# First-layer weights of an attention and two-FFN kernel: the shifted high word in a gapless tile of its own, joined with sign and low bits by one operation

## The chip, the core and the metric

One core of one Trainium2 chip. The metric is the device time of one execution in microseconds (us), with the median of three runs for the kernel before: 911.22 us (910.86 to 913.75).

## What is computed

Attention with 32 global and 512 local positions, 4 batches of 8 heads, a window of 32 around each local position; then two FFN layers on its 2176 rows of 512 columns:

```
x = attention(q_l, k_l, v_l, q_g, k_g, v_g)          # 2176 x 512
h = x @ moe_w_in;  x = (h * sigmoid(h)) @ moe_w_out  # 512 x 2048, 2048 x 512
h = x @ moe2_w_in; out = (h * cos(h)) @ moe2_w_out
```

The four weight matrices are float64 and have to become fp32 on the chip; the rest is fp32. Each fp32 product is made of three matmuls on a high and a low part of either operand.

## The kernel before

TensorE does each GEMM tile as `lo*xh`, `hi*xh`, `hi*xl` (`gemm1`, L491 to L493, into `ps_hid`; `gemm2` of the first layer, L558 to L560, into `ps_y`). The first layer works through tiles of tokens; tile 0 has 512 tokens and goes through 16 slices f of the hidden dimension. It needs all first-layer weights for the first time, so the conversion of these weights runs during tile 0: 32 chunks (16 slices, two parts each, 512 weights per partition), in the order in which the GEMMs want them. A chunk goes through these steps:

- `load_w1` (L113): a DMA brings 1024 words, low and high word of each float64 in turn, into a tile `raw`.
- `rebias` (L123): ScalarE multiplies the high words by a power of two in place (L125), so that a later shift by 3 gives the fp32 exponent; then it turns the low words into their top three bits, in place (L128). Both go over every other word.
- `to_f32` (L130): VectorE puts the sign of the high word into the low word (L136), then shifts the high word left by 3 and joins it with that (L140), into a gapless tile `w` out of the pool `stage`, tag "f", two buffers.
- `split_w_hi` (L153): ScalarE (L160) or, for the eight chunks in POOLED, GpSimd (L158) rounds `w` to the high part. `split_w_lo` (L163) subtracts on VectorE (L165), which frees `w`.

The weights of the second layer use the same two functions later, in chunks of 256, with one more shift on VectorE (L135). Tags "r" and "f" of `stage` (two buffers each) also hold those chunks' raw words, a batch's global values (`load_vg`, tag "f") and results on their way out (`finish`).

Beside the weights tile 0 carries the attention of further units of 256 positions: scores on TensorE (L243), masking and maximum on VectorE (L256, four instructions per unit, here called a **group**), exponentials on ScalarE (L266), transposes on VectorE (L196), global key parts on GpSimd (L202, L203), values on TensorE (`unit_values`, L335, L342). During tile 0 `gemm2` holds two of the four buffers `ps_a`, so one is free for a unit's values `ps_o` only when the group of the next unit has read its scores. Units 8 to 11 give four such groups in tile 0. VectorE also has `act` (L500) and `gl` (L535) for each slice f; ScalarE has the tanh (L499) and `gh` (L530).

The order of the work is a table of ticks (`at(rank, tick, function)`). From tick 0 to 35, which holds tile 0, a scheduler of the language puts each engine's instructions in order; before and after, they stand as recorded. Every engine works its own list in that order and waits in place.

Of the kernel before, what the change touches and what calls it, by code (L numbers as in the profile page):

```python
# [11 lines left out]
F32 = mybir.dt.float32  # L12
F32R = mybir.dt.float32r
I32 = mybir.dt.int32
U32 = mybir.dt.uint32
AF = mybir.ActivationFunctionType
ALU = mybir.AluOpType
# [23 lines left out]
ROUND = 12582912.0  # L41
REBIAS = 2.0**-112
SIGN = -(2**31)

TOP3 = 2.0**-29 * (1.0 - 2.0**-18)
TOP3_BIAS = -0.5 + 7.5 * 2.0**-18
# [3 lines left out]
def attention_then_two_ffn(  # L50
# [9 lines left out]
    nc = tc.nc  # L60
# [3 lines left out]
    stage = ctx.enter_context(tc.tile_pool(name="stage", bufs=2))  # L64
# [46 lines left out]
    W = {}  # L111

    def load_w1(f, part):  # L113
        raw = wts.tile([128, 1024], I32, tag=f"w{part}_{f}", name="raw")
        nc.sync.dma_start(out=raw, in_=w1[f, :, part * 1024 : part * 1024 + 1024])
        W[0, f, part] = raw.rearrange("p (n two) -> p n two", two=2)

    def load_w2_words(f, part):
        raw = stage.tile([128, 512], I32, tag="r", name="raw")
        nc.sync.dma_start(out=raw, in_=w2[f, :, part * 512 : part * 512 + 512])  # L120
        W[1, f, part] = raw.rearrange("p (n two) -> p n two", two=2)

    def rebias(ph, f, part):  # L123
        high = W[ph, f, part][:, :, 1].bitcast(F32)
        nc.scalar.activation(out=high, in_=high, func=AF.Copy, scale=REBIAS)  # L125
        if ph == 0:
            low = W[ph, f, part][:, :, 0]
            nc.scalar.activation(out=low, in_=low.bitcast(U32), func=AF.Copy, scale=TOP3, bias=TOP3_BIAS)  # L128

    def to_f32(ph, f, part):  # L130
        words = W[ph, f, part]
        n = words.shape[1]
        low, high = words[:, :, 0], words[:, :, 1]
        if ph == 1:
            nc.vector.tensor_scalar(out=low, in0=low, scalar1=29, scalar2=None, op0=ALU.logical_shift_right)  # L135
        nc.vector.scalar_tensor_tensor(  # L136
            out=low, in0=high, scalar=SIGN, in1=low, op0=ALU.bitwise_and, op1=ALU.bitwise_or
        )
        w = stage.tile([128, n], F32, tag="f", name="w")
        nc.vector.scalar_tensor_tensor(  # L140
            out=w.bitcast(I32), in0=high, scalar=3, in1=low, op0=ALU.logical_shift_left, op1=ALU.bitwise_or
        )
        W[ph, f, part] = w

    def store_w2(f, part):
        nc.sync.dma_start(out=w2f[f][part // 2][:, part % 2 * 256 : part % 2 * 256 + 256], in_=W.pop((1, f, part)))
# [449 lines left out]
    head, pre, gemm, pe, post = -20, 0, 10, 20, 40  # L596
# [6 lines left out]
    def begins(ph, t):  # L603
        return tick[seq.index((ph, t, 0))]
# [4 lines left out]
    def at(rank, i, fn, *args):  # L609
        plan.setdefault(i, []).append((rank, fn, args))  # L610
# [75 lines left out]
    for i, (need, f, part) in enumerate(chunks):  # L686
        s = min(need - SLACK, FIRST + i * (tick[NF] - 3 - FIRST) // (len(chunks) - 1))
        if i >= AHEAD:
            at(post, s - LOADS, load_w1, f, part)
        at(head + 6, s, rebias, 0, f, part)  # L690
        at(head + 7, s + 1, to_f32, 0, f, part)
        at(head + 10, s + 1, split_w_hi, 0, f, part)
        at(head + 6.5, s + 2, split_w_lo, 0, f, part)

# [3 lines left out]
    for i in range(4 * NF):  # L698
        s = free[i * len(free) // (4 * NF)]
        at(post, s - 2, load_w2_words, i // 4, i % 4)  # L700
        at(pre, s, rebias, 1, i // 4, i % 4)
        at(post - 1, s, to_f32, 1, i // 4, i % 4)
        at(pre, s + 1, store_w2, i // 4, i % 4)
    for f in range(NF):
        i = seq.index((0, len(SPANS) - 1, f))
# [6 lines left out]
    for i, (ph, t, f) in enumerate(seq):  # L712
        s = tick[i]
# [10 lines left out]
    for t, n in enumerate(size[1]):  # L724
        s = last if t == 0 else begins(1, t - 1)
# [19 lines left out]
    for n in range(5, EARLY):  # L745
        load_w1(*chunks[n - 5][1:])
        load_qk(n)
        load_v(n - 2)
    for n in range(EARLY - 2, EARLY):
        load_w1(*chunks[n - 3][1:])  # L750
        load_v(n)
# [90 lines left out]
```

## Time and profile before

| what | us |
|---|---|
| median of three runs (lowest, highest) | 911.22 (910.86, 913.75) |
| profiled execution, span from first to last instruction | 908.7 |
| TensorE matmul busy | 886.9 (98% of the span) |
| VectorE busy | 634.2 (70%) |
| ScalarE busy | 490.5 (54%) |
| GpSimd busy | 119.7 (13%) |

The page gives no time of the profiled execution beside its span; the median of the runs is 2.5 us above the span. Instruction rows of the trace give a start, a duration, and in brackets how long the engine was idle before and who ended that. An instruction of VectorE or ScalarE begins before the one ahead has ended, so what one costs is the distance from start to start, a little less than its duration. In tables of stretches PEclk is the granted TensorE clock as a share of full speed.

### The profile page before, as it was taken

How to read it: one execution, taken by the hardware profiler on the slowest of the kernel's cores; microseconds unless marked ns; L12 is line 12 of the kernel's file. 1: busy time of each engine (PE TensorE's matmuls, PEld its weight loads, DVE VectorE, ACT ScalarE, POOL GpSimd, SP SyncE). 2: the span in 40 equal slices, each digit the busy share in tenths (PEclk: the TensorE clock that was granted, in tenths of full speed). 3: DMA queues.
4: the chain of work that ended last, by engine and by line, in shares of the span. 5: the costliest groups of instructions: out<-in, count | busy, mean ns of one | idle time of the engine just before them, and what ended most of it. 6: DMA issues, size and time to landing. Idle time of an engine off the chain costs nothing.

```text
span 908.7 us, 15912 instructions
## 1 busy us (share of the span) xinstructions
PE 886.9 (98%) x5790; PEld 765.8 (84%) x5790; DVE 634.2 (70%) x1604; ACT 490.5 (54%) x1170; POOL 119.7 (13%) x147
## 2 busy tenths in 40 slices
PE   8899899999999999999999999999999999999998
PEld 5667678889888989999888889988889888888896
DVE  4799995688979677676488766666556656665654
ACT  4989843555644645444354465554445555444543
POOL 2220210021222212011155520000000000000000
PEclk9999989999999999999999999999999999999999
DMA  8968510566565664343546420000001000000100
GB/s 262 336 205 297 170 44 12 157 200 198 170 185 154 188 179 123 119 119 89 165 159 193 145 87 24 25 35 12 1 23 48 24 24 35 13 0 1 47 1 36
DMA packets 71839, 97.78 MB, mean 108 GB/s; under 512 B 22864, under 2 KB 38736, under 8 KB 71760
## 3 DMA queue, kind: packets, MB, share of 16 engines
q1 hardware_dynamic: 71760, 96.76, 34.3%
q8 instruction: 46, 0.75, 0.3%
q14 instruction: 33, 0.27, 0.1%
HBM read 79.43 MB, written 17.30 MB: 106 GB/s over the span
## 4 chain that ended last, share of the span: by engine, by line
PE 75%; DVE 10%; ACT 6%; DMA 2%; issue 1%; POOL 0%; SPq 0%; ACTq 0%; DVEq 0%
PE ps_hid L493 11%; PE ps_hid L491 11%; PE ps_hid L492 11%; PE ps_y L558 6%; PE ps_y L565 6%; PE ps_y L564 6%; PE ps_y L566 6%; PE ps_y L559 6%; PE ps_y L560 6%; PE ps_o L342 1%; DVE raw L136 1%; DVE gl L535 1%; PE ps_s L243 1%; DVE w L140 1%; ACT gh L530 1%
## 5 line engine op out<-in xcount | busy, mean ns | idle before, releaser
L493 PE MATMUL ps_hid<-xl,wt 128*128 128x512 f32 (+2 forms) x704 | 240.3, 341 | 0.0
L491 PE MATMUL ps_hid<-xh,wt 128*128 128x512 f32 (+2 forms) x704 | 240.2, 341 | 0.0
L492 PE MATMUL ps_hid<-xh,wt 128*128 128x512 f32 (+2 forms) x704 | 239.9, 341 | 0.0
L491 PEld LDWEIGHTS ps_hid<-xh,wt 128*128 128x128 f32 x704 | 133.0, 189 | 12.7 <-issue 0.4
L492 PEld LDWEIGHTS ps_hid<-xh,wt 128*128 128x128 f32 x704 | 133.0, 189 | 12.0
L493 PEld LDWEIGHTS ps_hid<-xl,wt 128*128 128x128 f32 x704 | 132.9, 189 | 10.3 <-DVE xl L355 0.3
L524 DVE TENSOR_TENSOR rest<-rest,ps_hid 128x384 f32<-128x384 f32 (+1 forms) x80 | 48.7, 608 | 132.8 <-ACT rest L520 132.7
L558 PE MATMUL ps_y<-gh,wt 128*128 128x256 f32 (+2 forms) x384 | 133.2, 347 | 0.0
L560 PE MATMUL ps_y<-gl,wt 128*128 128x256 f32 (+2 forms) x384 | 126.8, 330 | 0.3 <-DVE gl L535 0.3
L559 PE MATMUL ps_y<-gh,wt 128*128 128x256 f32 (+2 forms) x384 | 127.0, 331 | 0.0
L530 ACT CAST gh<-rest 128x384 fp32r<-128x384 f32 (+1 forms) x80 | 44.6, 558 | 122.4 <-PE ps_y L566 90.5
L564 PE MATMUL ps_y<-wt,gl 128*128 128x512 f32 x272 | 106.0, 390 | 1.7 <-DVE gl L535 1.7
L566 PE MATMUL ps_y<-wt,gh 128*128 128x512 f32 x272 | 106.7, 392 | 0.0
L565 PE MATMUL ps_y<-wt,gh 128*128 128x512 f32 x272 | 106.6, 392 | 0.0
L499 ACT ACTIVATE act<-ps_hid 128x256 f32<-128x256 f32 (+2 forms) x96 | 44.7, 466 | 89.6 <-PE ps_hid L493 89.5
L500 DVE SCALAR_TENSOR_TENSOR act<-act,ps_hid 128x256 f32<-128x256 f32 (+2 forms) x96 | 50.7, 528 | 56.3 <-ACT act L499 55.6
L558 PEld LDWEIGHTS ps_y<-gh,wt 128*128 128x128 f32 x384 | 73.1, 190 | 14.1 <-issue 6.5
L530 ACT CAST gh<-act 128x256 fp32r<-128x256 f32 (+2 forms) x96 | 47.6, 496 | 64.2 <-DVE act L500 42.5
L560 PEld LDWEIGHTS ps_y<-gl,wt 128*128 128x128 f32 x384 | 73.3, 191 | 6.2 <-DVE gl L535 1.0
L559 PEld LDWEIGHTS ps_y<-gh,wt 128*128 128x128 f32 x384 | 73.4, 191 | 4.9
L535 DVE TENSOR_TENSOR gl<-act,gh 128x256 fp32r<-128x256 f32 (+2 forms) x96 | 52.9, 551 | 28.6 <-ACT gh L530 27.2
L136 DVE SCALAR_TENSOR_TENSOR raw<-raw 128x256 int32<-128x256 int32 (+1 forms) x96 | 65.0, 682 | 5.1 <-ACT raw L125 1.0
(92 smaller groups left out, 1393.0 us busy)
## 6 DMA issues: line engine op xcount, KB each, us to landing
raw<-in_w_dram SPq DMA_DIRECT2D x32, 512.0 KB, 7.8
raw<-in_w_dram SPq DMA_DIRECT2D x64, 256.0 KB, 3.5
qk<-in_units_dram SPq DMA_DIRECT2D x32, 320.0 KB, 3.9
v<-in_units_dram SPq DMA_DIRECT2D x32, 256.0 KB, 3.5
w2f<-w SPq DMA_DIRECT2D x64, 128.0 KB, 3.0
w<-w2f SPq DMA_DIRECT2D x32, 256.0 KB, 2.9
gin<-in_glob_dram SPq DMA_DIRECT2D x16, 304.0 KB, 4.0
out_dram<-y SPq DMA_DIRECT2D x17, 256.0 KB, 2.1
```

Source lines behind the costliest of these rows:

```text
L136: nc.vector.scalar_tensor_tensor(out=low, in0=high, scalar=SIGN, in1=low, op0=ALU.bitwise_and, op1=ALU.bitwise_or)
L491: nc.tensor.matmul(h, lo[:, ws], xh[:, k, :], start=k == 0, stop=False)
L492: nc.tensor.matmul(h, hi[:, ws], xh[:, k, :], start=False, stop=False)
L493: nc.tensor.matmul(h, hi[:, ws], xl[:, k, :], start=False, stop=k == NP - 1)
L530: nc.scalar.copy(hi, g)
L535: nc.vector.tensor_tensor(out=lo, in0=g, in1=hi.bitcast(F32), op=ALU.subtract)
L558: nc.tensor.matmul(o, lo[:, ds_], gh, start=f == 0 and d % per == 0, stop=False, skip_group_check=True)
L559: nc.tensor.matmul(o, hi[:, ds_], gh, start=False, stop=False, skip_group_check=True)
L560: nc.tensor.matmul(o, hi[:, ds_], gl, start=False, stop=f == NF - 1, skip_group_check=True)
L564: nc.tensor.matmul(y[c], gl[:, cs], hi, start=f == 0, stop=False)
L565: nc.tensor.matmul(y[c], gh[:, cs], hi, start=False, stop=False)
L566: nc.tensor.matmul(y[c], gh[:, cs], lo, start=False, stop=f == NF - 1)
```

## The change

First-layer chunks get functions of their own. ScalarE now writes the scaled high words to a gapless tile `w` (L130), and the top three bits, as 16-bit values, into the lower half of the old high word, whose upper half still has the sign (L131). VectorE shifts `w` in place (L139) and joins it with sign and low bits, masked out of the high word in one operation (L140). `w` is now taken at ScalarE's step, from tag "r" and tag "f" in turn. Second-layer chunks are handled as before.

```diff
+SIGN_AND_LOW3 = SIGN + 7
...
-    def rebias(ph, f, part):
-        high = W[ph, f, part][:, :, 1].bitcast(F32)
+    def rebias_w1(f, part, room):
+        raw = W[0, f, part]
+        words = raw.rearrange("p (n two) -> p n two", two=2)
+        halves = raw.bitcast(U16).rearrange("p (n four) -> p n four", four=4)
+        w = stage.tile([128, 512], F32, tag=room, name="w")
+        nc.scalar.activation(out=w, in_=words[:, :, 1].bitcast(F32), func=AF.Copy, scale=REBIAS)
+        nc.scalar.activation(
+            out=halves[:, :, 2], in_=words[:, :, 0].bitcast(U32), func=AF.Copy, scale=TOP3, bias=TOP3_BIAS
+        )
+        W[0, f, part] = words[:, :, 1], w
+
+    def w1_to_f32(f, part):
+        marks, w = W[0, f, part]
+        bits = w.bitcast(I32)
+        nc.vector.tensor_scalar(out=bits, in0=bits, scalar1=3, scalar2=None, op0=ALU.logical_shift_left)
+        nc.vector.scalar_tensor_tensor(
+            out=bits, in0=marks, scalar=SIGN_AND_LOW3, in1=bits, op0=ALU.bitwise_and, op1=ALU.bitwise_or
+        )
+        W[0, f, part] = w
...
-        at(head + 6, s, rebias, 0, f, part)
-        at(head + 7, s + 1, to_f32, 0, f, part)
+        at(head + 6, s, rebias_w1, f, part, "rf"[i % 2])
+        at(head + 7, s + 1, w1_to_f32, f, part)
```

Later lines move down by 17: the masking instructions L256 are L273 now, `act` L500 is L517, `gl` L535 is L552, the tanh L499 is L516, the subtraction L165 is L182, the rounding L160 is L177.

The scheduler orders ticks 0 to 35 anew. VectorE's instructions by stretch (join before: L136 and L140; now shift L139 and join L140):

| stretch of VectorE's list | before: L136, L140, L165, L500 | now: L139, L140, L182, L517 |
|---|---|---|
| first chunk to group 1 | 16, 15, 13, 5 | 18, 17, 16, 6 |
| group 1 to group 2 | 4, 3, 5, 3 | 5, 4, 5, 2 |
| group 2 to group 3 | 4, 4, 4, 2 | 5, 6, 4, 2 |
| group 3 to group 4 | 4, 4, 4, 2 | 4, 4, 6, 2 |
| after group 4 | 4, 6, 6 | 0, 1, 1 |

VectorE between group 3 and group 4, from the `act` of one slice to that of the next, behind which group 4 stands. Before:

```order
L196 STREAM_TRANSPOSE tg_1633<-s_1534 32x4x32 x2
L500 SCALAR_TENSOR_TENSOR act_1618<-act_1618,ps_hid_1605 128x512
L196 STREAM_TRANSPOSE tg_1633<-s_1534 32x4x32 x2
L140 SCALAR_TENSOR_TENSOR w_1665<-raw_1423 128x512
L535 TENSOR_TENSOR gl_1638<-act_1618,gh_1631 128x512
L136 SCALAR_TENSOR_TENSOR raw_1456<-raw_1456 128x512
L165 TENSOR_TENSOR wt_1667<-w_1665,wt_1667 128x512
L140 SCALAR_TENSOR_TENSOR w_1713<-raw_1456 128x512
L136 SCALAR_TENSOR_TENSOR raw_1494<-raw_1494 128x512
L136 SCALAR_TENSOR_TENSOR raw_1544<-raw_1544 128x512
L165 TENSOR_TENSOR wt_1715<-w_1713,wt_1715 128x512
L500 SCALAR_TENSOR_TENSOR act_1686<-act_1686,ps_hid_1673 128x512
```

The same place now:

```order
L213 STREAM_TRANSPOSE tg_1634<-s_1535 32x4x32 x4
L517 SCALAR_TENSOR_TENSOR act_1619<-act_1619,ps_hid_1606 128x512
L140 SCALAR_TENSOR_TENSOR w_1785<-raw_1589,w_1785 128x512
L139 TENSOR_SCALAR w_1821<-w_1821 128x512
L139 TENSOR_SCALAR w_1849<-w_1849 128x512
L552 TENSOR_TENSOR gl_1639<-act_1619,gh_1632 128x512
L182 TENSOR_TENSOR wt_1827<-w_1785,wt_1827 128x512
L140 SCALAR_TENSOR_TENSOR w_1821<-raw_1622,w_1821 128x512
L140 SCALAR_TENSOR_TENSOR w_1849<-raw_1660,w_1849 128x512
L139 TENSOR_SCALAR w_1909<-w_1909 128x512
L182 TENSOR_TENSOR wt_1855<-w_1821,wt_1855 128x512
L182 TENSOR_TENSOR wt_1890<-w_1849,wt_1890 128x512
```

The second `act` (L517) and group 4 follow. The transposes now all stand ahead of the first `act`, and the chunks are further on: in the list before, the raw words 1423, 1456, 1494 and 1544 are in work here, now the last four but one.

ScalarE at the same place, between the exponentials of group 3 and the tanh whose `act` is above. Before:

```order
L266 ACTIVATE s_1534,st_1535<-s_1534,st_1535 128x160 x4
L353 CAST xh1_123<-ps_o_1562 128x256
L160 CAST wt_1596<-w_1594 128x512
L160 CAST wt_1629<-w_1627 128x512
L499 ACTIVATE act_1618<-ps_hid_1605 128x512
```

Now:

```order
L283 ACTIVATE s_1535,st_1536<-s_1535,st_1536 128x160 x4
L370 CAST xh1_123<-ps_o_1563 128x256
L131 ACTIVATE raw_1589<-raw_1589 128x512
L130 ACTIVATE w_1821<-raw_1622 128x512
L130 ACTIVATE w_1849<-raw_1660 128x512
L177 CAST wt_1791<-w_1754 128x512
L131 ACTIVATE raw_1622<-raw_1622 128x512
L131 ACTIVATE raw_1660<-raw_1660 128x512
L516 ACTIVATE act_1619<-ps_hid_1606 128x512
```

Before, ScalarE had done all its conversions by here; now parts of three chunks' conversions stand ahead of this tanh, and each L130 can begin only when a buffer of `w` is free again. Ahead of group 1 ScalarE's list has 37 conversions now (L130, L131), where it had 43 (L125, L128).

## Rows read from the trace of the kernel before

**Rows 1.** The page: span, part 1 (busy), part 4 (chain by engine).

```profile
span 908.7 us, 15912 instructions
...
PE 886.9 (98%) x5790; PEld 765.8 (84%) x5790; DVE 634.2 (70%) x1604; ACT 490.5 (54%) x1170; POOL 119.7 (13%) x147
...
PE 75%; DVE 10%; ACT 6%; DMA 2%; issue 1%; POOL 0%; SPq 0%; ACTq 0%; DVEq 0%
```

**Rows 2.** Stretches between the groups: from:to, length, busy and (instructions) by engine, PEclk.

```profile
33.09:81.27 48.18, 44.52 (x297) 33.56 (x298) 43.39 (x91) 43.63 (x97) 10.48 (x18) 1.00 0.79 268
81.27:97.23 15.96, 14.82 (x107) 11.43 (x105) 15.68 (x39) 14.76 (x34) 2.94 (x3) 1.00 0.84 285
97.23:112.51 15.28, 13.43 (x85) 10.38 (x85) 14.79 (x37) 12.17 (x28) 2.63 (x2) 1.00 0.39 124
112.51:129.16 16.65, 14.66 (x84) 11.36 (x84) 14.79 (x37) 7.67 (x19) 2.62 (x2) 0.90 0.15 40
129.16:160.00 30.84, 30.13 (x164) 25.15 (x165) 20.68 (x47) 12.35 (x28) 2.02 (x2) 0.94 0.08 22
```

**Rows 3.** Waits of TensorE, 43 to 150 us: us in total, times, longest.

```profile
PE ps_o L335 <- DVE st L256: 5.2, 3, 2.0
```

**Rows 4.** Timeline of TensorE around three waits: start, us, instruction.

```profile
97.94 0.47 PE L335 MATMUL ps_o<-pgt,vst 96*128 96x256 f32 x2 [1.41 <-DVE st L256]
...
100.24 0.39 PE L491 MATMUL ps_hid<-xh,wt 128*128 128x512 f32 x1
...
113.22 0.50 PE L335 MATMUL ps_o<-pgt,vst 96*128 96x256 f32 x2 [1.85 <-DVE st L256]
...
117.23 0.39 PE L491 MATMUL ps_hid<-xh,wt 128*128 128x512 f32 x1
117.46 0.40 PE L492 MATMUL ps_hid<-xh,wt 128*128 128x512 f32 x1
...
129.87 0.47 PE L335 MATMUL ps_o<-pgt,vst 96*128 96x256 f32 x2 [1.98 <-DVE st L256]
...
134.37 0.40 PE L491 MATMUL ps_hid<-xh,wt 128*128 128x512 f32 x1
```

**Rows 5.** Timeline of VectorE: start, us, instruction.

```profile
62.62 0.69 DVE L136 SCALAR_TENSOR_TENSOR raw<-raw 128x512 int32<-128x512 int32 x1
63.23 0.69 DVE L535 TENSOR_TENSOR gl<-act,gh 128x512 fp32r<-128x512 f32 x1
...
74.80 0.50 DVE L406 TENSOR_SCALAR sg<-sg,stg 128x544 f32<-128x544 f32 x1
75.22 0.69 DVE L165 TENSOR_TENSOR wt<-w,wt 128x512 fp32r<-128x512 f32 x1
...
189.68 0.29 DVE L135 TENSOR_SCALAR raw<-raw 128x256 int32<-128x256 int32 x1
```

**Rows 6.** VectorE by line, 20 to 150 us: count, busy us, mean ns, idle before.

```profile
L277 DVE TENSOR_SCALAR s<-s,st 128x160 f32<-128x160 f32 x38 | 9.0, 299 | 0.2
...
L196 DVE STREAM_TRANSPOSE tg<-s 32x128 f32<-32x128 f32 x16 | 4.8, 298 | 0.2
```

**Rows 7.** VectorE between groups 2 and 3, and 3 and 4: `act` and the wait ahead of it.

```profile
103.88 0.69 DVE L500 SCALAR_TENSOR_TENSOR act<-act,ps_hid 128x512 f32<-128x512 f32 x1 [0.40 <-ACT act L499]
...
120.85 0.69 DVE L500 SCALAR_TENSOR_TENSOR act<-act,ps_hid 128x512 f32<-128x512 f32 x1 [1.78 <-ACT act L499]
```

**Rows 8.** A VectorE instruction beside one of GpSimd, timelines.

```profile
107.19 1.79 DVE L136 SCALAR_TENSOR_TENSOR raw<-raw 128x512 int32<-128x512 int32 x1
...
106.81 1.62 POOL L203 TENSOR_TENSOR pgt<-tg,pgt 32x512 fp32r<-32x512 f32 x1
```

**Rows 9.** ScalarE: its conversions by line (20 to 150 us), and its waits (43 to 131 us).

```profile
L125 ACT ACTIVATE raw<-raw 128x512 f32<-128x512 f32 x32 | 21.6, 674 | 0.3 <-DMA raw<-in_w_dram 0.3
...
ACT act L499 <- PE ps_hid L493: 6.4, 6, 4.0
```

More of the change, by code (lines that the diff above doesn't have):

```diff
@@ L14 @@
 I32 = mybir.dt.int32
+U16 = mybir.dt.uint16
 U32 = mybir.dt.uint32
@@ L115, in load_w1 @@
         nc.sync.dma_start(out=raw, in_=w1[f, :, part * 1024 : part * 1024 + 1024])
-        W[0, f, part] = raw.rearrange("p (n two) -> p n two", two=2)
+        W[0, f, part] = raw
     def load_w2_words(f, part):
@@ L121, in load_w2_words, with rebias_w2, w2_to_f32 @@
         W[1, f, part] = raw.rearrange("p (n two) -> p n two", two=2)
-    def rebias(ph, f, part):
-        high = W[ph, f, part][:, :, 1].bitcast(F32)
-        nc.scalar.activation(out=high, in_=high, func=AF.Copy, scale=REBIAS)
[L126 to L132, printed above, removed]
+    def rebias_w1(f, part, room):
[16 more added lines that the diff above has]
+        W[0, f, part] = w
+    def rebias_w2(f, part):
+        high = W[1, f, part][:, :, 1].bitcast(F32)
+        nc.scalar.activation(out=high, in_=high, func=AF.Copy, scale=REBIAS)
+    def w2_to_f32(f, part):
+        words = W[1, f, part]
         low, high = words[:, :, 0], words[:, :, 1]
-        if ph == 1:
-            nc.vector.tensor_scalar(out=low, in0=low, scalar1=29, scalar2=None, op0=ALU.logical_shift_right)
+        nc.vector.tensor_scalar(out=low, in0=low, scalar1=29, scalar2=None, op0=ALU.logical_shift_right)
         nc.vector.scalar_tensor_tensor(
@@ L138, in to_f32 @@
         )
-        w = stage.tile([128, n], F32, tag="f", name="w")
+        w = stage.tile([128, 256], F32, tag="f", name="w")
         nc.vector.scalar_tensor_tensor(
@@ L142, in to_f32 @@
         )
-        W[ph, f, part] = w
+        W[1, f, part] = w
     def store_w2(f, part):
@@ L700, in attention_then_two_ffn @@
         at(post, s - 2, load_w2_words, i // 4, i % 4)
-        at(pre, s, rebias, 1, i // 4, i % 4)
-        at(post - 1, s, to_f32, 1, i // 4, i % 4)
+        at(pre, s, rebias_w2, i // 4, i % 4)
+        at(post - 1, s, w2_to_f32, i // 4, i % 4)
         at(pre, s + 1, store_w2, i // 4, i % 4)
```

## The prediction

> **What bounds the kernel now.** I read the page first, then the table of stretches, then the waits of TensorE, then the timelines around them. The page [rows 1] says that TensorE is busy for 98% of a span of 908.7 us and has 75% of the chain that ended last; VectorE has 10% of that chain. The conversion of the first-layer weights touches only the time up to 150 us, so I cut that time at the four groups of masking instructions [rows 2]. From the first chunk's VectorE work (33.09) to group 3 (112.51) VectorE is nearly always busy: 15.68 of 15.96 us between groups 1 and 2, 14.79 of 15.28 between 2 and 3. In that time TensorE waits for it. Its waits for `ps_o` come to 5.2 us in three pieces [rows 3], all ended by a masking instruction: a unit's values need a buffer that the next unit's group frees, and the group stands behind conversions in VectorE's list. The pieces are 1.41, 1.85 and 1.98 us [rows 4]. Behind the second and third TensorE's clock was lower: 0.90 and 0.94 of full speed in these two stretches, against 1.00 in the stretches that begin earlier [rows 2]. The price of that is in the rows 4. From the start of the values to the next `ps_hid` it took 2.30 us at 97.94 with five `ps_y` matmuls between them, 4.01 at 113.22 with six, 4.50 at 129.87 with eight. At 0.23 us per further matmul (117.23 to 117.46) the two would be 2.53 and 2.99, so the clock cost 1.5 us each time. All that this change can win there is thus some 5.2 + 3.0 = 8.2 us. After group 4 TensorE waits for nothing until 150 us.
>
> **What the change does, step by step.** On **VectorE** 32 instructions of the form L136 go and 32 shifts L139 come. L136 costs 0.61 us from start to start [rows 5], I use 0.60, as for every one of VectorE's 512-wide instructions with two inputs. A shift by a constant is known from L135, 0.29 us for 256 words at every other place; two other forms with one tensor input are L406, 0.50 us for 544 elements [rows 5], and L277, 0.30 us for 160 [rows 6]. These two differ by 0.20 us over 384 elements, 0.52 ns each. With that slope L135 comes to 0.29 + 256 x 0.52 ns = 0.42 us at 512, and since the next instruction starts 0.08 us before one ends (0.69 against 0.61, and 0.50 against 0.42 [rows 5]), it holds the next up for 0.34. Ends: 0.34, and 0.60 if the shift takes as long as the forms with two inputs; on the way lies 0.40, from L406 scaled down. I take 0.34, because L135 is the same operation. The new join L140 reads every other word on one input and none on the other; it replaces one that did so on both, so 0.60 again.
>
> The rows show no penalty for every other word: L136, with all operands so, has 0.61, and the gapless `gl` behind it 0.60 [rows 5]. The Trainium skill ("Vector Engine (DVE) Microarchitecture Reference", section "Measured stream behaviour on trn2") puts a stream that jumps at each element at 1.73 ns per column where one source does it; the join would then be an estimated 0.89 us and the whole 32 x 0.29 = 9 us dearer. The trace contradicts that for this spacing.
>
> By itself the swap frees 32 x 0.26 = 8.3 us of VectorE. But what counts is how much work stands **ahead of each group**, and the scheduler has moved conversions forward: the table of counts shows it, and after group 4 there are 2 chunk instructions where there were 16. With 0.60 and 0.34:
>
> - First chunk to group 1: before 49 instructions of 0.60, 29.4 us; now 39 of 0.60 and 18 of 0.34, 29.5 us. Change 0.
> - Groups 1 to 2: before 15 x 0.60 = 9.0; now 11 x 0.60 + 5 x 0.34 = 8.3. Change -0.7.
> - Groups 2 to 3: before 14 x 0.60 = 8.4; now 12 x 0.60 + 5 x 0.34 = 8.9. Of the 0.5 more, 0.4 goes into VectorE's wait ahead of `act` [rows 7], which was idle. Change +0.1.
> - Groups 3 to 4: a wait of 1.78 us for the tanh stands in the middle [rows 7], so only what lies behind it counts. From `act` to the next `act`, both counted, before ten instructions and two transposes (0.30 each [rows 6]), 6.6; now nine and three shifts, 6.4. The transposes that feed GpSimd also stand ahead of the wait now, so that a part of what L203 costs VectorE falls into idle time. L203 beside a two-input instruction stretched that from 0.69 to 1.79 [rows 8]; I count 0.2 of the 1.1. Change -0.4.
>
> Sum: -1.0 us, all of it as shorter waits of TensorE for `ps_o`. What was freed beyond that falls behind group 4, where no wait of TensorE is left to shorten.
>
> On **ScalarE** the two conversions stay two instructions of 0.67 us, 32 times [rows 9]. L130 writes without gaps, L131 writes 16-bit values; nothing in the trace writes such values at this spacing, so I bound each by 0.1 us either way (a sixth of L125), 6.4 us in all, and take nothing. The cover is the 6.4 us in which the tanh waited for TensorE [rows 9]; if it is gone, the tanh is late, which is the second rival. L131 must also wait for L130 on its own engine. **DMA**: the loads of the raw words are the same; the queue of SP has one global-values load (`vraw`) some loads further ahead, which waits for a buffer "f" and holds up the loads behind it; these are issued six ticks early, and ScalarE's L125 waited 0.3 us in all for a load [rows 9]. I cost it at nothing. GpSimd's list is unchanged.
>
> The sum against the profiled execution: 908.7 - 1.0 = 907.7 us span. The page shows no own time for it, so I add the 2.5 us by which the runs' median exceeds the span: **910.2 us**.
>
> **Rivals.** *The relief reaches TensorE (faster).* If the group instructions come up earlier than my counts say, the waits go in one piece and the clock does not fall: a wait of 1.41 us left it at 1.00, waits of 1.85 and 1.98 did not [rows 2, 4]. The third wait at 1.98 - 0.4 lies between these. Losing that fall alone gives -2.5 us; halving all waits and losing both falls gives -2.6 - 3.0 = -5.6, 905.6; the floor is -8.2, 903.0. For it: ScalarE's list has 37 conversions ahead of group 1 where it had 43. Against it: VectorE's counts.
>
> *ScalarE is tied to VectorE (slower).* L130 may begin only when the subtraction four chunks back has freed its buffer; before, ScalarE worked ahead in `raw` itself, as far as loads had come. If an L130 waits, the tanh behind it is late, `act` waits on VectorE, and the group behind that. One L130 (0.67, as L125 [rows 9]) and one subtraction (0.60) ahead of the tanh are 1.3 us; in each of four stretches 5.2, with one more fall of the clock 1.5, less the sum's 1.0: +5.7, **916.9**. It decides once VectorE's idle time ahead of `act` grows beyond 0.40 and 1.78 [rows 7]. For it: ScalarE was busy 14.76 of 15.96 us between groups 1 and 2 [rows 2]. Against it: `w` has four buffers where it had two.
>
> *The shift does not run at two elements a step.* Then each is 0.60, and 32 x 0.26 = 8.3 us come on top ahead of group 4: 918 at most. L135 speaks against it; I give it 3 in 100, within the slower case.
>
> **Chances and range.** Forecast (within 0.3%, that is 2.7 us, about what can be told apart here): 0.45. Relief: 0.32. Slower: 0.23. The range leaves out the far end of the relief and that of the slower case: 904.5 to 915.5. The forecast's own range is 908.5 to 913.9.
>
> **What would show it.** The shift at 0.40 to 0.45 us; three waits for `ps_o` ended by L273 of some 0.7, 1.9 and 1.6 us, the middle one with a low clock behind it; conversions over soon after group 4; group 4 within 2 us of 129. Wrong would be: no wait above 1 us (relief), or the tanh waiting ahead of `ps_hid`'s end for a buffer and VectorE idle ahead of `act` for more than 2 us (tied).

## The result: slower, and the profile after

The changed kernel takes 920.34 us (median of six runs, 918.11 to 921.96) where the kernel before, in runs beside it, took 911.04: a ratio of 1.0101, with a 95% interval of 1.0086 to 1.0117. The prediction was 910.2 us, with a range up to 915.5. The profiled execution took 920.74 us, with a span of 919.0 where it was 908.7 [rows 1].

The page of the changed kernel, the same three parts as in [rows 1]:

```profile
span 919.0 us, 15931 instructions
...
PE 892.2 (97%) x5790; PEld 769.6 (84%) x5790; DVE 624.7 (68%) x1604; ACT 509.7 (55%) x1170; POOL 117.8 (13%) x147
...
PE 76%; DVE 10%; ACT 9%; issue 2%; DMA 2%; SPq 1%; POOL 0%; ACTq 0%; DVEq 0%; POOLq 0%
```

VectorE lost 9.5 us of work, which was the aim. ScalarE gained 19.2 us, for the same 1170 instructions, and its part of the chain went from 6% to 9%. TensorE's same 5790 matmuls took 5.3 us longer, and it stood idle 5.0 us longer (919.0 - 892.2 against 908.7 - 886.9): together the 10.3 us. The low-word conversion of the kernel before, by line (20 to 170 us; the high-word one is in [rows 9]):

```profile
L128 ACT ACTIVATE raw<-raw 128x512 int32<-128x512 uint32 x32 | 21.3, 669 | 0.0
```

The two conversions of the changed kernel, from the same view:

```profile
L131 ACT ACTIVATE raw<-raw 128x512 uint16<-128x512 uint32 x32 | 42.3, 1381 | 0.3
L130 ACT ACTIVATE w<-raw 128x512 f32<-128x512 f32 x32 | 20.9, 675 | 2.9 <-DVE wt L182 2.9
```

L131 has as many elements as L128 had, and takes 1381 ns where L128 took 669. From start to start it holds ScalarE for 1.1 us (at 95.06 two L131 in a row last 2.52 together), not 0.57: 0.55 x 32 = 18 us more. L130 is no faster for its gapless output. What VectorE did, by line and from its timeline, and what it waited for (0 to 180 us, the changed kernel and then the one before):

```profile
L140 DVE SCALAR_TENSOR_TENSOR w<-raw,w 128x512 int32<-128x512 int32 x32 | 23.0, 729 | 1.8 <-ACT raw L131 1.7
...
L139 DVE TENSOR_SCALAR w<-w 128x512 int32<-128x512 int32 x32 | 14.6, 485 | 0.6 <-ACT w L130 0.6
```

```profile
99.44 0.76 DVE L139 TENSOR_SCALAR w<-w 128x512 int32<-128x512 int32 x2
```

```profile
DVE act L517 <- ACT act L516: 24.8, 15, 4.5
```

```profile
DVE act L500 <- ACT act L499: 13.2, 10, 3.4
```

Two shifts in a row end after 0.76 us, so one holds the next up for 0.34, as forecast. But VectorE now waits 24.8 us for the tanh, where it waited 13.2. The stretches between the groups, to be read beside [rows 2] (columns: from:to, length, then busy and instructions of TensorE, its weight loads, VectorE, ScalarE and GpSimd, and the granted clock):

```profile
32.76:88.41 55.65, 48.84 (x314) 35.90 (x314) 44.29 (x102) 53.03 (x95) 9.72 (x18) 0.94 0.71 235
88.41:107.31 18.90, 17.04 (x103) 13.51 (x103) 14.81 (x40) 17.09 (x32) 2.82 (x3) 0.82 0.73 245
107.31:124.17 16.86, 13.64 (x86) 10.57 (x86) 14.93 (x40) 16.20 (x31) 2.52 (x2) 0.98 0.35 111
124.17:141.24 17.07, 15.91 (x85) 12.32 (x85) 14.55 (x39) 14.31 (x27) 2.03 (x2) 0.81 0.08 22
```

VectorE, busy all but 0.3 to 0.5 us of the second and third stretch before, is now idle 4.1 and 1.9 us there; ScalarE is busy 53.0 of 55.7 us ahead of group 1, and 16.2 of 16.9 us between groups 2 and 3. It has become the engine that ends last. Group 4 comes at 141.24 where it came at 129.16. Waits of TensorE, one in the first stretch and four behind the groups, from its timeline:

```profile
36.83 0.50 PE L352 MATMUL ps_o<-pgt,vst 96*128 96x256 f32 x2 [1.71 <-ACT pgt L315]
...
89.12 0.63 PE L448 MATMUL ps_og<-pgt,vst 96*128 96x32 f32 x4 [1.73 <-DVE st L273]
...
108.03 0.47 PE L352 MATMUL ps_o<-pgt,vst 96*128 96x256 f32 x2 [1.87 <-DVE st L273]
...
124.88 0.77 PE L352 MATMUL ps_o<-pgt,vst 96*128 96x256 f32 x2 [3.21 <-DVE st L273]
...
141.94 0.47 PE L352 MATMUL ps_o<-pgt,vst 96*128 96x256 f32 x2 [1.15 <-DVE st L273]
```

In the stretches of the waits at 36.83, 89.12 and 124.88 the granted clock is 0.94, 0.82 and 0.81: a part of each ran at 1.2 GHz, not 2.4. The wait at 36.83 is for ScalarE; in the kernel before, its counterpart (35.98) lasted 1.10 us, and the clock of that stretch was 1.00 [rows 2].

### The profile page after: what moved, and what is told of

It reads as the page before. It is cut to its first block, busy times and chain, and to the rows that moved or that the text cites. A ratio compares the mean times of both kernels' runs of the same rounds, so it can differ in the third digit from the quotient of the medians.

```text
span 919.0 us, 15931 instructions
## 1 busy us (share of the span) xinstructions
PE 892.2 (97%) x5790; PEld 769.6 (84%) x5790; DVE 624.7 (68%) x1604; ACT 509.7 (55%) x1170; POOL 117.8 (13%) x147
## 4 chain that ended last, share of the span: by engine, by line
PE 76%; DVE 10%; ACT 9%; issue 2%; DMA 2%; SPq 1%; POOL 0%; ACTq 0%; DVEq 0%; POOLq 0%
PE ps_hid L508 11%; PE ps_hid L510 11%; PE ps_hid L509 11%; PE ps_y L575 6%; PE ps_y L583 6%; PE ps_y L582 6%; PE ps_y L581 6%; PE ps_y L577 6%; PE ps_y L576 6%; PE ps_s L260 2%; ACT raw L131 2%; PE ps_o L359 2%; DVE gl L552 1%; PE ps_t L325 1%; ACT gh L547 1%
## 5 line engine op out<-in xcount | busy, mean ns | idle before, releaser
L508 PEld LDWEIGHTS ps_hid<-xh,wt 128*128 128x128 f32 x704 | 133.5, 190 | 12.9 <-PE ps_sg L395 0.4
L517 DVE SCALAR_TENSOR_TENSOR act<-act,ps_hid 128x256 f32<-128x256 f32 (+2 forms) x96 | 50.7, 528 | 69.9 <-ACT act L516 69.3
L516 ACT ACTIVATE act<-ps_hid 128x256 f32<-128x256 f32 (+2 forms) x96 | 45.2, 471 | 88.4 <-PE ps_hid L510 88.4
L552 DVE TENSOR_TENSOR gl<-act,gh 128x256 fp32r<-128x256 f32 (+2 forms) x96 | 51.6, 538 | 30.6 <-ACT gh L547 29.2
L525 ACT ACTIVATE turns<-ps_hid 128x384 f32<-128x384 f32 (+1 forms) x80 | 42.6, 533 | 36.7 <-PE ps_hid L510 36.5
```

The lines of the kernel that those rows point to most:

```text
L508: nc.tensor.matmul(h, lo[:, ws], xh[:, k, :], start=k == 0, stop=False)
L517: nc.vector.scalar_tensor_tensor(out=a, in0=a, scalar=1.0, in1=h, op0=ALU.add, op1=ALU.mult)
L552: nc.vector.tensor_tensor(out=lo, in0=g, in1=hi.bitcast(F32), op=ALU.subtract)
```

## The experiments

The theory after this reading: the 16-bit write of L131 is dear, and that alone makes the loss. Against it stood my second rival (ScalarE tied through the four buffers of `w`), an effect of the new order, and contention.

**1. The low bits as 32-bit values again.**

```diff
-            out=halves[:, :, 2], in_=words[:, :, 0].bitcast(U32), ...
+            out=words[:, :, 0], in_=words[:, :, 0].bitcast(U32), ...
```

> The changed kernel with one edit: L131 writes its three low bits as 32-bit integers back into the low word, as before, and no longer as 16-bit values into the high word. The join still reads the high word, so the three lowest bits of each first-layer weight are not the right ones. Everything else (gapless w, the shift, one join, four buffers) stays. Price theory (the 16-bit write costs ScalarE 1.38 us where the 32-bit one cost 0.67, and that is the whole loss): L131 near 0.67 us, VectorE's wait for the tanh back from 24.8 to under 12 us, groups 2 to 4 within 2 us of 97, 112.5 and 129, time 907 to 912 us, as my sum of 910.2 had it. Buffer theory (L130 in the buffer of w ties ScalarE to VectorE's subtraction): L131 near 0.67, but L130 still waits for L182 and the tanh stays late; 915 to 920. Order theory (the groups stand behind more conversions in VectorE's list than I counted): VectorE busy throughout without waiting for the tanh, groups late; 914 to 918.

Measured: 911.57 us, ratio 1.0014 (0.9992 to 1.0037). L131 takes 680 ns; groups 2 to 4 come at 98.83, 114.81 and 131.05, the last two just outside the 2 us that I had given them. The loss is gone, so the write has a part in it. But VectorE still waited 22.4 us for the tanh, where I had under 12: idle time of VectorE by itself doesn't measure the loss. The join no longer waits for L131 here (1.7 us in the changed kernel, none here) and the scheduler made other lists, so this run alone doesn't isolate the price.

**2. As much ScalarE work in the kernel before.**

```diff
             nc.scalar.activation(out=low, in_=low.bitcast(U32), func=AF.Copy, scale=TOP3, bias=TOP3_BIAS)
+            nc.scalar.activation(out=low, in_=low.bitcast(U32), func=AF.Copy, scale=1.0)
```

> The kernel before with one ScalarE instruction more per chunk: a copy of the low word onto itself, 512 elements, 32 times, estimated from L128 at 0.67 us each, 0.57 from start to start, 18 us of ScalarE in all, about what L131 takes more than L128 did (32 x (1.38 - 0.67) = 23 us by duration, 32 x 0.55 = 18 by starts). VectorE's three-step conversion stays as it was. Price theory: ScalarE has no room for this, the tanh comes late; 918 to 923 us with VectorE's wait for the tanh over 20 us. Buffer theory: nothing ties ScalarE in this kernel and it was ahead by the conversions in raw; the 18 us fall into its idle time, 910 to 914.

Measured: 910.24 us, ratio 1.0001 (0.9986 to 1.0015). Some 18 us more on ScalarE cost nothing. My price theory failed here as it stood: work of this size is not a loss by itself. Either the structure of the kernel before absorbs it, or its order, which the scheduler made with the copy in it: ScalarE begins 18 chunks ahead of group 1, then 4, 4, 4 and 3, where in the kernel before it begins 22, 6, 4 and none.

**3. The forms by themselves, 512 elements.** Rows of eight instructions behind the end of the changed kernel.

> The changed kernel with rows of eight instructions of one form each appended behind its end, when no other engine works; its time is of no interest. 512 elements each on ScalarE: 32-bit to 32-bit at every other word (the form of L128), 32-bit to 16-bit at every fourth half (the form of L131), to 16-bit without gaps, to 32-bit without gaps, from gapless to 16-bit at every fourth half, from float, float to float, to 16-bit at every other half, to bfloat16 at every fourth half, from 16-bit to 16-bit at every fourth half; on VectorE the shift at every other word, the 16-bit shift at every fourth half, the shift without gaps. Price by form: the form of L131 takes 1.33 to 1.45 us alone as it did in the kernel, that of L128 0.67. If so, price by width: every form with 16-bit output is near 1.35, gaps or not; price by place: 16-bit without gaps 0.67 and at every fourth half 1.35. Rival, contention: alone, the form of L131 takes 0.67 to 0.8 us, and the rest in the kernel comes from VectorE's and the DMA's traffic.

Measured: ScalarE's from windows that tell the forms apart (8 bytes from element to element, in 32 and in 16 bits, then 16 bits gapless), and VectorE's by line (L831 16 bits at every fourth half, L829 32 bits at every other word, L833 32 bits gapless):

```profile
L806 ACT ACTIVATE dst<-src 128x512 int32<-128x512 uint32 x6 | 3.9, 652 | 1.8 <-DVE dst L797 1.6
```

```profile
L806 ACT ACTIVATE dst<-src 128x512 uint16<-128x512 uint32 x6 | 8.0, 1333 | 0.2
```

```profile
L806 ACT ACTIVATE dst<-src 128x512 uint16<-128x512 uint32 x2 | 1.3, 654 | 0.1
```

```profile
L831 DVE TENSOR_SCALAR dst<-src 128x512 uint16<-128x512 uint16 x8 | 5.9, 734 | 18.5 <-ACT dst L806 18.3
...
L829 DVE TENSOR_SCALAR dst<-src 128x512 int32<-128x512 int32 x8 | 3.4, 429 | 61.1 <-ACT dst L806 60.9
L833 DVE TENSOR_SCALAR dst<-src 128x512 int32<-128x512 int32 x8 | 3.4, 427 | 0.3
```

Alone, with all else idle, L131's form takes 1333 ns: contention is out. It takes the same with a gapless input, from float, from 16-bit or to bfloat16 (1335 to 1344 ns), so it is the output. And 16 bits as such cost nothing: gapless, 654 ns. It is 16-bit values at every fourth half.

**4. The dear write on VectorE.**

```diff
-        nc.scalar.activation(
-            out=halves[:, :, 2], in_=words[:, :, 0].bitcast(U32), func=AF.Copy, scale=TOP3, bias=TOP3_BIAS
-        )
...
+        nc.vector.tensor_scalar(
+            out=halves[:, :, 2], in0=halves[:, :, 1], scalar1=13, scalar2=None, op0=ALU.logical_shift_right
+        )
```

> The changed kernel with L131 taken from ScalarE and done by VectorE: a 16-bit shift right by 13 of the upper half of the low word, written to the lower half of the high word, ahead of the shift. The result is the same. ScalarE loses 32 x 1.10 = 35 us by starts, VectorE gets 32 instructions. Price theory with a shift of 0.34 by starts: VectorE's conversion is 0.34 + 0.34 + 0.60 = 1.28 us beside 1.20 in the kernel before, ScalarE's 0.6 beside 1.2; nothing waits for the tanh; 907 to 913 us. If VectorE pays for the 16-bit write as ScalarE does, twice (0.68 to 0.9 us): 32 x 0.4 = 13 us more on VectorE, the groups late, 916 to 922. Buffer theory: L130 still waits for L182, 914 to 920.

Measured: 921.82 us, ratio 1.0108 (1.0075 to 1.0141), as expected for a VectorE that pays too.

```profile
L135 DVE TENSOR_SCALAR raw<-raw 128x512 uint16<-128x512 uint16 x32 | 26.7, 835 | 0.2 <-ACT w L130 0.2
```

Here L130 waited 13.8 us for the buffers, since ScalarE ran ahead; that is idle time of an engine with room, and says nothing on the loss.

**5. The changed kernel with a cheap write, all lists held.** The next two runs put the other price on a fixed order: each has the lists of the kernel that it is made from on all five engines, instruction for instruction, which also shows that the scheduler does not tell the two writes apart.

```diff
-            out=halves[:, :, 2], in_=words[:, :, 0].bitcast(U32), ...
+            out=raw.bitcast(U16)[:, 0:512], in_=words[:, :, 0].bitcast(U32), ...
```

> The changed kernel with its lists on all five engines unchanged, instruction for instruction, and one thing different: L131 writes its 512 16-bit values without gaps into the first kilobyte of the raw tile, not into every fourth half. The low three bits of the first-layer weights are then not the right ones, nor the sign of the first 128 in each row. In the row of forms that write took 0.65 us, the one at every fourth half 1.33. Price theory (the dear write alone, on this order, is the loss): L131 at 0.66 us, 905 to 912 us, groups 2 to 4 near 98, 113 and 129. Theory of structure (the dear write costs little, the four buffers and the order that was planned for them do it): 915 us or more, groups still 8 us or more late.

Measured: 906.89 us, ratio 0.9953 (0.9937 to 0.9969): faster than the kernel before, by 4.1 us, and 13.5 below the changed one. The line of the write, the page, and the stretches up to group 4:

```profile
L131 ACT ACTIVATE raw<-raw 128x512 uint16<-128x512 uint32 x32 | 20.7, 670 | 0.3
```

```profile
PE 885.0 (98%) x5790; PEld 764.7 (84%) x5790; DVE 624.1 (69%) x1604; ACT 490.8 (54%) x1170; POOL 119.2 (13%) x147
```

```profile
0.00:81.41 81.41, 75.36 (x616) 53.05 (x616) 61.92 (x205) 62.47 (x160) 20.34 (x52) 1.00 0.82 270
81.41:96.41 15.00, 14.04 (x104) 11.07 (x103) 14.78 (x40) 13.85 (x32) 2.87 (x3) 1.00 0.93 318
96.41:111.30 14.89, 13.62 (x86) 10.57 (x86) 14.82 (x39) 13.30 (x31) 2.54 (x2) 1.00 0.37 122
111.30:125.87 14.57, 13.40 (x85) 10.38 (x85) 14.46 (x39) 11.66 (x27) 2.03 (x2) 1.00 0.17 46
```

The spans differ by 13.9 us (905.1 and 919.0). TensorE's busy time makes 7.2 of it (892.2 - 885.0, the same matmuls at a lower clock), its idle time 6.7. The clock is 1.00 in all four stretches here, and from group 4 to 170 us. These rows also give the mechanism: with no wait of TensorE above 1.3 us, a stretch between groups lasts some 15 us, and ScalarE has 13.85, 13.30 and 11.66 us of work in it. It runs 5, 5 and 4 of the L131 there; at 0.55 us more each that makes 16.6, 16.1 and 13.9 us. The first two no longer fit. The third would, yet in the changed kernel it lasts 17.07 us: TensorE is busy 15.91 us of it, not 13.40, so the lower clock makes the difference there. Ahead of group 1 it is 18 x 0.55 = 9.9 us, and group 1 came 7.0 later. L130 waited 6.1 us for the buffers of `w` in this, the fastest run, and 2.9 in the changed kernel: the buffers are not the cause.

**6. The kernel before with the dear write, all lists held.**

```diff
-            nc.scalar.activation(out=low, in_=low.bitcast(U32), ...
+            nc.scalar.activation(out=half, in_=low.bitcast(U32), ...
...
-            out=low, in0=high, scalar=SIGN, in1=low, op0=ALU.bitwise_and, op1=ALU.bitwise_or
+            out=low, in0=(low, high)[ph], scalar=(7, SIGN)[ph], in1=low, op0=ALU.bitwise_and, op1=(ALU.bitwise_and, ALU.bitwise_or)[ph]
```

> The kernel before with its lists on all five engines unchanged and the dear write put in: L128 writes 16-bit values to the lower half of the low word, at every fourth half; L136 masks the low word to three bits where it joined the sign to them, so the sign of the first-layer weights is dropped. L128 at 1.38 us. If the price alone makes the loss, whatever the structure: 917 to 922 us. If ScalarE's lead in this kernel (22 conversions begun ahead of group 1 against 13 subtractions done) takes it up, as the 18 us of the run with an extra copy were taken up: 909 to 913 us; but there the order was planned with the extra copy in it, here it isn't, so between the two (913 to 917) would say that the order has a part.

In the edit, `half` is the lower half of each low word.

Measured: 923.28 us, ratio 1.0135 (1.0112 to 1.0158), 1.3 us above the range of the case in which the price alone makes the loss. L128 takes 1363 ns, and group 4 comes at 140.35. The stretch between groups 1 and 2:

```profile
87.41:108.64 21.23, 17.56 (x106) 13.70 (x104) 15.74 (x38) 19.89 (x36) 2.57 (x3) 0.84 0.64 216
```

ScalarE, with 14.76 us of work here in the kernel before [rows 2], has 19.89. The structure of the kernel before doesn't absorb the dear write either, so run 2 was saved by its order.

**7. The changed structure with a cost that the scheduler sees.**

```diff
-            out=halves[:, :, 2], in_=words[:, :, 0].bitcast(U32), ...
+            out=words[:, :, 0], in_=words[:, :, 0].bitcast(U32), ...
         )
+        nc.scalar.activation(out=words[:, :, 0], in_=words[:, :, 0].bitcast(U32), func=AF.Copy, scale=1.0)
-        W[0, f, part] = words[:, :, 1], w
+        W[0, f, part] = words[:, :, 0], w
```

> The changed kernel's structure (w without gaps in four buffers, shift, one join that waits for L131), with ScalarE as busy as in it but with a cost that the scheduler knows when it makes the order: L131 writes 32-bit values to the low word at 0.67 us, and a copy of the low word onto itself follows, 0.57 from start to start. The join reads the low word, so the sign of the first-layer weights is dropped. If the loss comes from an order planned for a cheap L131: 909 to 913 us, as the kernel before with the same copy. If it comes from ScalarE's work in a structure where it cannot run ahead: 917 to 922 us, with the tanh waited for some 20 us and L130 waiting for L182.

Measured: 910.40 us, ratio 0.9988 (0.9971 to 1.0004).

```profile
83.30:99.10 15.80, 14.75 (x107) 11.37 (x105) 14.62 (x37) 14.46 (x33) 2.69 (x3) 1.00 0.88 285
99.10:114.25 15.15, 13.62 (x86) 10.57 (x86) 14.02 (x36) 13.82 (x32) 2.08 (x2) 1.00 0.22 67
114.25:129.42 15.17, 13.63 (x86) 10.57 (x86) 14.03 (x36) 13.83 (x32) 2.10 (x2) 1.00 0.18 49
```

ScalarE now begins 17 chunks ahead of group 1, 4 in each stretch between groups, and 3 behind group 4, where the changed kernel has 19, 6, 4, 3 and none. So spread, its work is 14.46, 13.82 and 13.83 us and fits everywhere. The same ScalarE time costs 13.5 us on an order that doesn't allow for it (the changed kernel against run 5); with one that does, the kernel stays level with the one before, 3.5 us above run 5. Runs 6 and 7 both drop the signs of the first-layer weights and lie 12.9 us apart, so the changed values do not make the times.

**8. The old form for 20 chunks, the new one for 12.** Edit: `rebias` and `to_f32` of the kernel before for i below 20, the changed functions from there.

> A version that may beat both: the first 20 chunks as in the kernel before, the last 12 as in the changed one, correct result. In the kernel before ScalarE was busy 44.1 of 48.7 us and 14.8 of 16.0 ahead of group 2, but 12.2 of 15.3 and 7.7 of 16.7 behind it, so 12 x 0.55 = 6.6 us more fit there, while VectorE saves 12 x 0.26 = 3.1 us where TensorE waits for it (waits of 1.85 and 1.98 us and the clock behind them). If ScalarE has the room: 906 to 910 us. If the dear write makes the tanh late there too: 912 to 916.

Measured: 915.58 us, ratio 1.0048 (1.0028 to 1.0068), near the upper end of the worse case. The stretch between groups 1 and 2:

```profile
82.33:100.30 17.97, 16.22 (x106) 12.74 (x106) 15.69 (x39) 9.79 (x22) 2.94 (x3) 0.91 0.72 243
```

This loss can't be put down to the dear write alone: this stretch has one of the 12, ScalarE has room, and it still lasts 2.0 us longer than before, at a lower clock. What the mixed order does there stays open.

**9 and 10. Conversions due later, by one constant, in either kernel.**

```diff
-    LEAD, SLACK, LOADS, AHEAD, FIRST, CUT = 9, 3, 6, 8, -4, 36
+    LEAD, SLACK, LOADS, AHEAD, FIRST, CUT = 9, 3, 6, 8, -2, 36
```

> The changed kernel, correct, with the dear write, and one constant of the plan changed: FIRST from -4 to -2, so that conversions are due later. ScalarE's list then has 6, 8, 10, 13, 15, 17, 20, 22, 25, 28, 30, 32 conversions begun ahead of the first twelve tanhs, where the changed kernel had 7, 9, 11, 14, 16, 18, 21, 23, 27, 29, 31, 32 and the run with the known cost 7, 8, 10, 13, 15, 17, 19, 21, 23, 25, 27, 29. If the place of the conversions among the tanhs makes the loss, this goes a third to a half of the way: 913 to 917 us. If the order has no such part, or the slack in front of the chunks is needed more: 918 to 923.

> The control: the kernel before with the same constant, FIRST -2. ScalarE's list has 7, 9, 12, 15, 18, 21, 24, 27, 30, 32 conversions ahead of the first ten tanhs, where it had 7, 10, 11, 16, 18, 22, 25, 27, 30, 32. With cheap writes the conversions are not late and not early enough to matter: 909 to 912.5 us. If the constant by itself moves the time, it shows here, by 3 us or more either way, and the run beside it must be read against that.

Measured: 919.62 us for the changed kernel, ratio 1.0106 (1.0089 to 1.0123), and 908.53 for the one before, 0.9976 (0.9957 to 0.9994). The first misses the 913 to 917 that I had for a loss made by the place of the conversions, and lies in the other case (the order has no such part, or the slack ahead of the chunks is needed more). The second is 0.5 us below its range: the constant by itself wins 1.6 us, less than the 3 us that would have mattered. In the changed kernel group 1 came 2.9 us earlier (85.48), but the conversions that were put off went into the stretches behind group 2 (5 and 4 chunks begun, where the changed kernel has 4 and 3), and none behind group 4. The stretch between groups 2 and 3:

```profile
102.76:120.82 18.06, 17.12 (x88) 13.23 (x88) 15.74 (x41) 17.10 (x32) 2.03 (x2) 0.81 0.27 84
```

ScalarE is busy 17.10 of 18.06 us there, and the clock falls there instead. Beside run 7 this speaks for room and not for later work: no stretch with more than it holds.

**11. The forms, 256 elements, by spacing.**

> The changed kernel with rows of eight instructions of one form each behind its end, 256 elements, nothing else running. ScalarE, 32-bit input at every other word: 32-bit output gapless, at every 2nd, 3rd and 4th word; 16-bit output gapless, at every 2nd, 3rd, 4th and 8th half. VectorE: the 16-bit shift into gapless, every 2nd and every 4th half, the last also from a gapless input; the 32-bit shift at every 2nd and every 4th word. In the row of 512 elements, 16-bit output took 0.65 us gapless, 0.775 at every 2nd half, 1.335 at every 4th, and 32-bit 0.65 at every 2nd word. If the count of elements stepped over decides: 32-bit at every 4th word is as dear as 16-bit at every 4th half (twice the gapless one), at every 3rd between. If the bytes stepped over decide (8 bytes dear, 4 nearly not): contradicted already by 32-bit at every 2nd word, unless small elements alone pay: then all 32-bit forms are at one price, near 0.43 us at 256. 16-bit at every 8th half: no dearer than every 4th if the price saturates at two steps per element, 4 times the gapless if it grows on. VectorE: if it pays like ScalarE, every 2nd half near the gapless, every 4th 1.6 times.

Measured (ScalarE: L803 to L806 write 32 bits gapless, at every 2nd, 3rd and 4th word, L807 to L811 write 16 bits gapless, at every 2nd, 3rd, 4th and 8th half; VectorE: L812 to L814 write 16 bits gapless, at every 2nd and 4th half, L815 as L814 from a gapless input, L816 and L817 32 bits at every 2nd and 4th word):

```profile
L811 ACT ACTIVATE dst<-src 128x256 uint16<-128x256 uint32 x8 | 10.7, 1334 | 0.3
L810 ACT ACTIVATE dst<-src 128x256 uint16<-128x256 uint32 x8 | 6.1, 768 | 0.3
L806 ACT ACTIVATE dst<-src 128x256 int32<-128x256 uint32 x8 | 5.2, 650 | 0.3
L809 ACT ACTIVATE dst<-src 128x256 uint16<-128x256 uint32 x8 | 5.0, 628 | 0.3
L805 ACT ACTIVATE dst<-src 128x256 int32<-128x256 uint32 x8 | 4.3, 539 | 0.3
L808 ACT ACTIVATE dst<-src 128x256 uint16<-128x256 uint32 x8 | 3.9, 488 | 0.3
L814 DVE TENSOR_SCALAR dst<-src 128x256 uint16<-128x256 uint16 x8 | 3.6, 452 | 0.3
L815 DVE TENSOR_SCALAR dst<-src 128x256 uint16<-128x256 uint16 x8 | 3.6, 451 | 0.3
...
L804 ACT ACTIVATE dst<-src 128x256 int32<-128x256 uint32 x8 | 3.4, 427 | 0.3
L807 ACT ACTIVATE dst<-src 128x256 uint16<-128x256 uint32 x8 | 3.4, 427 | 0.3
L817 DVE TENSOR_SCALAR dst<-src 128x256 int32<-128x256 int32 x8 | 3.1, 393 | 0.3
L813 DVE TENSOR_SCALAR dst<-src 128x256 uint16<-128x256 uint16 x8 | 2.5, 312 | 0.3
L816 DVE TENSOR_SCALAR dst<-src 128x256 int32<-128x256 int32 x8 | 2.4, 295 | 0.3
L812 DVE TENSOR_SCALAR dst<-src 128x256 uint16<-128x256 uint16 x8 | 2.4, 294 | 48.1 <-ACT dst L811 47.8
```

The price grows with the count of elements stepped over, and it does not saturate, but the count alone doesn't set it: I had one price for either width at every 4th place, and it is 650 ns for 32 bits and 768 for 16. On ScalarE 32 bits are free up to every 2nd word, then 0.11 us more for each further word; 16 bits cost a little at every 2nd half (488) and 0.14 us for each further half up to the 8th. At the same 8 bytes from element to element 32 bits cost 427 ns and 16 bits 768. VectorE pays of the same kind: 294 to 452 at every 4th half, 295 to 393 at every 4th word.

**12. The dear write on GpSimd.**

```diff
-        nc.scalar.activation(
-            out=halves[:, :, 2], in_=words[:, :, 0].bitcast(U32), func=AF.Copy, scale=TOP3, bias=TOP3_BIAS
-        )
+        nc.gpsimd.tensor_scalar(
+            out=halves[:, :, 2], in0=words[:, :, 0].bitcast(U32), scalar1=TOP3, scalar2=TOP3_BIAS, op0=ALU.mult, op1=ALU.add
+        )
```

> The changed kernel with L131 moved from ScalarE to GpSimd as a multiply and add with a 16-bit result, the same place in memory, correct result. The last place for the dear write: ScalarE loses 32 x 1.1 = 35 us by starts, VectorE keeps its saving, GpSimd (18 to 20 us busy between 30 and 140 us; L175, 512 elements, 0.63 us) gets 32 instructions. If GpSimd writes them at 0.65 to 1.3 us and VectorE is not held up beside it: 904 to 908 us, as the run with the gapless write (906.9) or better, since ScalarE is freer. If VectorE's instructions stretch beside GpSimd's as L136 did beside L203 (1.79 us for 0.69), say by 0.5 us in 32 places: 16 us more on VectorE, 915 to 925. If GpSimd is slow with a 16-bit result at every fourth half (over 3 us each, 100 us in all): chunks late, TensorE waits for wt, over 930.

Measured: 934.60 us, ratio 1.0250 (1.0225 to 1.0276): above the range of the case with stretched instructions, and not for the reason of the case above 930 (over 3 us on GpSimd).

```profile
L131 POOL TENSOR_SCALAR raw<-raw 128x512 uint16<-128x512 uint32 x32 | 48.7, 1523 | 41.9 <-ACT w L130 31.2 <-issue 5.9 <-DVE st L273 3.6
```

```profile
L140 DVE SCALAR_TENSOR_TENSOR w<-raw,w 128x512 int32<-128x512 int32 x32 | 28.5, 899 | 0.3
...
L139 DVE TENSOR_SCALAR w<-w 128x512 int32<-128x512 int32 x32 | 24.3, 778 | 0.0
```

GpSimd takes 1523 ns each, and VectorE's instructions stretch beside it: the shift from 485 to 778 ns, the join from 729 to 899, together 15 us over 32 chunks. The subtraction and `gl` stretch too, and VectorE's busy time is 650.3 us, 25.6 above the changed kernel: it is busy 19.02 of 19.15 us between groups 1 and 2 and has become the engine without room. No version that puts the 16-bit value in its place came below the kernel before.

## Why the prediction was wrong

**The step that failed is the term on ScalarE**: "the two conversions stay two instructions of 0.67 us", each bounded by 0.1 us. The operation, the count of elements and the bytes between them were those of L128, and I priced L131 by that; the width of the output was the one thing that had changed, no row showed it, and my bound of 0.1 us came from no row of such a write. It measured 1381 ns, 0.55 us more from start to start than L128, in all 18 us, nearly three times the 6.4 us that I had allowed for both lines together. The cover was the other half of the mistake: 6.4 us in which the tanh waited, taken over 88 us, where ScalarE's room has to be read stretch by stretch. [Rows 2] had it: 14.76 of 15.96 us busy between groups 1 and 2. And with the cheap write on the same lists (run 5) the loss is gone.

**VectorE's terms were right.** The shift is 0.42 us where nothing holds it up and 0.34 from start to start, as taken (its mean in the kernel is 485 ns). Nor was there a penalty for every other word: VectorE's 32-bit shift of 512 elements takes 429 ns at every other word, read and written, and 427 gapless (run 3). The Trainium skill ("Vector Engine (DVE) Microarchitecture Reference", section "Measured stream behaviour on trn2") gives full rate only to streams in runs of at least two adjacent words. These rows contradict that at every 2nd word; at every 4th the rows of run 11 (393 ns for 256 elements, where every 2nd takes 295) agree that a jumping output pays.

**The sum was too small, in the direction of the first rival.** With lists held and the write cheap (run 5), the span is 3.6 us below that of before, not 1.0. The clock is 1.00 up to 170 us, so both falls behind the waits, which I had priced at 3.0 us and given to the rival "the relief reaches TensorE" (905.6), did go. But the size hangs on the order: run 1, with the same work and other lists, is not measurably faster than before.

**The second rival had the place and not the mechanism.** The tanh was late, `act` waited on VectorE and the groups came late, as it said. The reason was the price of an instruction on ScalarE, not the wait for a buffer of `w`. And its price was too low: I had counted one fall of the clock, where the clock fell in the first stretch, the second and the fourth. TensorE's longer busy time is a good half of the loss. I had also gone by the length of a single wait to tell whether the clock falls. That does not hold here: behind the wait of 1.73 us (89.12) the stretch has 0.82, behind that of 1.87 (108.03) it has 0.98. And I had looked for waits of TensorE from 43 us on only, which left out the one at 36.83.

**The rival of a slow shift** is out; its sum, 910.2 + 8.3, should have read 918.5 and not 918. The DMA queue did not show as a cost on ScalarE: the 2.9 us of idle time ahead of L130 are all put down to L182, and L131 has 0.3 us.

## What to carry to other kernels

A new width or spacing of an output is a new form: price it from a row of that form, or give it the bounds of the dearest row there is, on every engine that it could go to. Write narrow values without gaps; written into the half of a wider word they cost double here (1333 against 654 ns). And where a scheduler makes the order, a price that it does not know can cost far more than the same work in its plan (here 13.5 us against 3.5): compare an engine's work with the length of each stretch, not with its idle time over the whole.

## What was not expected of the hardware

On ScalarE the price of an output grows with the number of elements stepped over: 16-bit values at every 2nd, 4th and 8th half take 488, 768 and 1334 ns for 256 elements, 32-bit values at every 2nd and 4th word 427 and 650. A write of 16 bits every 8 bytes is thus dearer than one of 32 bits at the same addresses. VectorE does likewise (452 ns for 16 bits, 295 for 32). GpSimd took 1523 ns for 512 elements beside VectorE's work; alone it was not measured.
